# One fused attention and gated-MLP kernel: three late loads moved in the load queue, later transfers planned on one shared wire, and a new order of all work

## The chip, the cores and the metric

The kernel runs on one core of a Trainium2 chip. The core has five engines with a queue of instructions each: TensorE (PE, matrix products into PSUM), VectorE (DVE), ScalarE (ACT), GpSimd (POOL) and SyncE (SP, which here only issues DMA transfers). Each engine runs its instructions in the order in which they are recorded and waits at an instruction until what it needs is there. The metric is the device time of one execution in microseconds (us). The time before is 220.81 us, the median of three runs (220.67 to 221.25).

## What is computed

The input x has 2048 tokens of 512 numbers in bfloat16. The reference, cut to what matters:

```python
x = A_x
xn = _layernorm(x, axis=-1)
s = _A_ref(xn, A_wqkv, A_wo)
g = _silu(_B_ref(xn, B_w_gate, B_w_up, B_w_down))
return x + s * g
```

`_A_ref` is a dilated local attention: q, k and v are products of xn with three 512x512 weights, split into 32 heads of 16; each token attends to 8 tokens, itself and the seven at distances 2, 4, ... 14 before it (those before the start are masked); softmax; then a product with the 512x512 weight wo. `_B_ref` is a gated MLP: gelu(xn w_gate) * (xn w_up), both 512x1792, then a product with the 1792x512 weight w_down, and silu of that.

## The kernel before

The tokens are worked on in four blocks of 512 (j = 0 to 3), each of four tiles of 128. For each block there are these stages:

- Layer normalization on DVE or ACT, and transposition so that the 512 features lie on partitions (tile `xnT`). Block 0 is transposed on PE and copied; blocks 1 to 3 by four DMA transpositions each, issued by SP (line 344, planner's names `copy4` to `copy15`).
- q, k, v: products of `xnT` with the weights. For block 0 by tile of 128 tokens (line 492), for the others in twelve groups of four matmuls of 512 tokens (line 429). ACT evicts each from PSUM (line 440), SP or POOL stores it to DRAM (line 447), and it is loaded again in another layout, heads on partitions (q at line 551, k at 569, v at 587).
- Logits on DVE: products of q with shifted windows of k (`prod`, lines 619 and 692), folds that sum over the 16 numbers of a head (line 705; one large fold in each later block is an adding DMA from POOL, line 714), maximum and difference (727, 733), exp on ACT (746), sum, reciprocal and share on DVE (752 to 762). In block 0 part of the sum runs on PE (`red0`, line 652).
- Values on DVE: four products `pv` a block (line 785), five adds, of which the first two of the four inner ones are adding DMAs (line 808). The result is `o_sb`. It goes to DRAM in four stores (line 941) and comes back transposed as `oT_sb` (line 950).
- Gate and up products: 28 groups of four matmuls a block (line 842), gelu and a copy on ACT (858, 866), the gate product on DVE (line 880, names `geglu`).
- Down products: `y_ps`, 14 matmuls a token tile in cuts of 4, 4, 4 and 2 (line 906); silu on ACT (line 924). Token tiles 0 and 1 share one PSUM tile of two banks, `ps_y`; tiles 2 and 3 take a bank each of the pool "F".
- Output: four matmuls a token tile (line 969), eviction (983), gate by silu (993, or 1020 in the last block), addition of x and store (996 and 1001, or 1026 and 1032).

The PSUM pool "F" has six banks for everything but the two-bank tile "L" (block 0's logits sums and each block's first two y tiles). The products of the gate wait in three buffers of the pool "gl", q, k and v in two buffers each, evicted q, k, v in five ("vst"), hT in one.

The order of the work is not written out. `Kernel` makes a list of about 850 operations with an engine, an estimated duration, needs, buffers and a priority. `schedule` (a list scheduler that runs when the kernel is built) walks them: at each step it picks, over all engines, the operation that can start earliest, ties within 0.05 us going to the lower priority number. The result is one global sequence, and instructions are recorded in it. Durations and costs steer only this order; at run time the engines wait on semaphores for data, buffers and, for each DMA queue, for the transfer eight before it. `slack` adds time to an estimated arrival, and so moves an operation later in the order. The priorities hold a base for each stage and block (`N`, `S`, `V`, `Q`, `F`, `Y`, `O` in `PARAMS`) and, before, a random offset of at most 1.0 from a seed.

Transfers are planned with two wires, one for SP's queue and one for POOL's, by bytes and a rate each, plus a fixed time. The first loads (`loads`) stand at the front of SP's queue: x of block 0 in tiles, q, k and v weights, x of block 1, gate and up weights in halves, x of block 2, the down weights (1792 KB), x of block 3 and the output weights (512 KB each).

Of the kernel before, what the change touches and what calls it, by code (L numbers as in the profile page):

```python
# [16 lines left out]
P = 128  # L17
H = 32
DH = 16
# [9 lines left out]
B, S, D, DF = 1, 2048, 512, 1792  # L29
# [3 lines left out]
TPB = TQ // P  # L33
# [18 lines left out]
PARAMS = dict(  # L52
    sums=(2, 3), ladd=2, ln_act=4, warm=4, slack=1.93, jitter=(8555, 1.0), N=[53.5, -4.6, 83.1, 89.8],
    S=[60.5, 102.4, 90.7, 136.5], V=[57.8, 104.8, 237.5, 47.1], Q=[-7.2, 49.5, -16.0, 37.2],
    F=[1.1, 76.5, 194.5, 255.4], Y=[64.5, 107.9, 241.7, 272.5], O=[82.0, 180.6, 272.0, 282.7], lsum=(0,),
    vsum=(0, 1),
)


class Op:  # L60
    __slots__ = ("name", "eng", "dur", "need", "emit", "take", "use", "prio", "table", "bytes",
                 "start", "done", "end", "n", "slack", "mode")

    def __init__(self, name, eng, dur, need, emit, take=(), use=(), prio=0.0, table=None, nbytes=0,
                 slack=0.0, mode="full"):
# [4 lines left out]
        self.mode = mode  # L70


def schedule(ops, pools):
# [16 lines left out]
    table, mode = None, "full"  # L90
    lanes, lane = {e: [0.0] * 8 for e in ("SP", "POOL")}, {"SP": 0, "POOL": 0}
    wire = {"SP": 0.0, "POOL": 0.0}
    ready = {e: [] for e in clock}
# [6 lines left out]
    while any(ready.values()):  # L100
# [26 lines left out]
        e = o.eng  # L127
# [4 lines left out]
        if o.bytes:  # L132
            clock[e] = t + o.dur
            wire[e] = max(wire[e], t + o.dur / 2) + o.bytes / DMA_RATE[e]
            end = wire[e] + DMA_FIXED + (DMA_CROWDED if e == "POOL" and t < LOADED else 0.0)
            lanes[e][lane[e]] = end
            lane[e] = (lane[e] + 1) % 8
        else:
            if o.table and o.table != table:
                t += TABLE  # L140
                table = o.table
            if e == "PE" and o.mode != mode:
                t += SWITCH
                mode = o.mode
            clock[e] = t + o.dur
            end = clock[e] + LAT[e]
# [19 lines left out]
class Kernel:  # L166
# [52 lines left out]
    def layernorm(self, j):  # L219
        base = self.when("N", j)  # L220
        for tt in range(TPB):
# [117 lines left out]
            if j:  # L339

                def cross(t=t, tt=tt, j=j):
                    if tt == 0:
                        self.new(f"xT{j}", [P, NC, TQ], BF16, "xnT")
                    self.nc.sync.dma_start_transpose(
                        out=self.t[f"xT{j}"][:, :, tt * P : (tt + 1) * P], in_=self.t[f"xn{t}"][:]
                    )

                self.op(f"copy{t}", "SP", 0.8, [f"norm{t}"] + ([f"copy{t - tt}"] if tt else []), cross,
                        take=[("xT", f"xT{j}")] if tt == 0 else [], use=[f"xn{t}", f"xT{j}"], prio=prio,
                        nbytes=P * D * 2)  # L350
                continue
# [63 lines left out]
    def qkv(self, j):  # L415
# [6 lines left out]
        for which, c in groups:  # L422
# [21 lines left out]
            def store(j=j, which=which, c=c, key=key):  # L444
# [7 lines left out]
                    use=["ps_" + key, "st_" + key], prio=0.0)  # L452
            self.op(f"st_{key}", *(("SP", 0.4) if which < 2 else ("POOL", 1.0)), [f"ev_{key}"], store,
                    use=["st_" + key], nbytes=128 * 1024)
            n += 1
# [4 lines left out]
    def halo(self, base):  # L460
# [13 lines left out]
        self.op("halo0", "POOL", 0.2, [], fill, take=[("k", "k0")], use=["k0"], prio=base - 50.0)  # L474
        self.op("st_k0", "SP", 0.5, ["ev_k0_3"], tail, use=["k0"], nbytes=256 * 1024, prio=5.0)

# [5 lines left out]
    def qkv_tiles(self, base):  # L482

        for t in range(TPB):
            for which in range(3):
# [51 lines left out]
                if which == 2:  # L537
                    self.op(f"st_v0_{t}", "POOL", 1.0, [f"ev_v0_{t}"], store, use=[f"vst0_{t}"],
                            nbytes=128 * 1024)
        self.v_loads(0)  # L540

    def q_loads(self, j):
        for tq in range(TPB):

            def load(j=j, tq=tq):
                if tq == 0:
# [10 lines left out]
            self.op(f"ldq{j}_{tq}", "SP", 0.6, need, load, take=[("q", f"q{j}")] if tq == 0 else [],  # L557
                    use=[f"q{j}"], prio=1.0, nbytes=260 * 1024)

    def k_loads(self, j):  # L560
        for tq in range(TPB):

            def load(j=j, tq=tq):
                if tq == 0:
# [12 lines left out]
            self.op(f"ldk{j}_{tq}", "SP", 0.6, need, load, take=[("k", f"k{j}")] if tq == 0 else [],  # L577
                    use=[f"k{j}"], prio=1.0, nbytes=290 * 1024)

    def v_loads(self, j):  # L580
        for tq in range(TPB):
# [14 lines left out]
            self.op(f"ldv{j}_{tq}", "POOL", 1.0, need, load, take=[("v", f"v{j}")] if tq == 0 else [],  # L596
                    use=[f"v{j}"], prio=1.0, nbytes=290 * 1024)

# [82 lines left out]
    def logits(self, j):  # L681
# [3 lines left out]
        for i in range(W // 2):  # L685
# [30 lines left out]
            for n, dur in ((8, 1.135), (4, 0.6), (2, 0.33), (1, 0.33)):  # L716
                if n == 8 and i in self.par["lsum"]:
                    last = self.op(f"fold{j}_{i}_8", "POOL", 1.0, [last], fold_dma, use=[pair],
                                   prio=base + 4 * i + 4.5, nbytes=P * DH * P * 2)
                    continue  # L720
# [57 lines left out]
    def values(self, j):  # L778
# [22 lines left out]
        for i in range(W // 2):  # L801
# [8 lines left out]
            if i in self.par["vsum"]:  # L810
                nm = self.op(f"vadd{j}_0_{i}", "POOL", 1.0, [nm], within_dma, use=[f"pv{j}_{i}"],
                             prio=base + k + 2.5, nbytes=P * DH * P * 2)
# [122 lines left out]
    def turned(self, j):  # L935

        for tq in range(TPB):
# [7 lines left out]

            self.op(f"sto{j}_{tq}", "SP", 0.6, [self.o_ready], store, use=[f"o{j}"], nbytes=340 * 1024, prio=-20.0)

        def load(j=j):
# [4 lines left out]

        self.op(f"ldo{j}", "SP", 0.6, [f"sto{j}_{tq}" for tq in range(TPB)], load, take=[("oT", f"oT{j}")],
                use=[f"oT{j}"], nbytes=512 * 1024, prio=-20.0)

    def out(self, j):
# [31 lines left out]
        if j < NJ - 1:  # L989
# [10 lines left out]
            def store(j=j):  # L1000
# [7 lines left out]
            self.op(f"add{j}", "POOL", 1.0, [f"gate{j}"], add, use=[f"s16{j}"], prio=20.0,  # L1008
                    nbytes=P * TPB * D * 2)
            self.op(f"store{j}", "SP", 0.35, [f"add{j}"], store, use=[f"s16{j}"], nbytes=P * TPB * D * 2)  # L1010
            return
        for tt in range(TPB):
            spans = [(0, 320), (320, D)] if tt == TPB - 1 else [(0, D)]
            for si, (n0, n1) in enumerate(spans):
# [27 lines left out]
                else:  # L1042
# [3 lines left out]
                self.op(f"store{sfx}", "SP", 0.35, [f"add{sfx}"], store, use=[f"s16{j}"],  # L1046
                        nbytes=P * (n1 - n0) * 2)


    def loads(self, src):  # L1050
# [45 lines left out]
        for i, (name, fn, nbytes) in enumerate(seq):  # L1096
            self.op(name, "SP", 0.35, [], fn, prio=-1000.0 + i, nbytes=nbytes)


def plan(par=PARAMS, pools=POOLS, src=(None,) * 6):  # L1100
    k = Kernel(par)
    k.loads(src)
    k.build()
    seed, spread = par["jitter"]
    rng = random.Random(seed)
    for o in k.ops:
        if o.eng in ("PE", "DVE", "ACT") and o.prio > -40.0:
            o.prio += spread * (2.0 * rng.random() - 1.0)
    order, k.slot = schedule(k.ops, pools)
# [108 lines left out]
```

## Time and profile before

| what | value |
|---|---|
| median of three runs | 220.81 us |
| the profiled execution's own time | 220.55 us |
| its span (first to last instruction) | 218.8 us |
| TensorE busy | 208.8 us, 95% |
| VectorE busy | 182.5 us, 83% |
| ScalarE busy | 154.9 us, 71% |
| GpSimd busy | 41.9 us, 19% |
| moved by DMA | 36.02 MB, mean 165 GB/s |
| mean granted clock of TensorE | 0.988 |

The time of an execution holds the span and about 1.7 us around it. All positions in time below are microseconds from the span's start. The busy share of an engine is a mean over stages with different limits, so the stages are looked at one by one: which wait ends last there. "SPq" is SP's queue of DMA issues, "PEld" the load of weights into PE, which overlaps its products. A view of waits names for each engine and line what released it. The chain is followed back from the last instruction, at each step to what released it.

### The profile page before, as it was taken

To read this page: it belongs to the slowest core of one execution; us is meant where nothing else is said; L and a number is where in the kernel's file an instruction comes from. 1 tells how busy PE (TensorE), PEld (TensorE's weight loads), DVE (VectorE), ACT (ScalarE), POOL (GpSimd) and SP (SyncE) were. 2 spreads that over 40 slices of the span, in tenths; PEclk is the share of its full clock that TensorE was granted. 3 is DMA by queue.
4 is the path that set the end of the run, shared out by engine and by line. 5 is a ranking of instruction groups with operands and counts; after the bars stand their busy time and mean duration, and the time that the engine had idled before them with its cause. 6 is when DMAs were issued, how large, how long until landed. Compare 5 with 4: busy or idle time off the path is not lost.

```text
span 218.8 us, 3109 instructions
## 1 busy us (share of the span) xinstructions
PE 208.8 (95%) x1108; PEld 99.3 (45%) x1108; DVE 182.5 (83%) x211; ACT 154.9 (71%) x265; POOL 41.9 (19%) x76
## 2 busy tenths in 40 slices
PE   7999999999399999999999999999999999999991
PEld 2896444444134444444444444444444444444440
DVE  5595995589941999999999999999999999994114
ACT  3588999998766888897734599767644897464351
POOL 5044310203314432240001144120101001101000
PEclk9999999999969999999999999999999999999998
DMA  5999999127999999928245869991075006905552
GB/s 159 363 382 371 323 283 182 26 71 171 234 208 195 256 218 251 166 51 148 96 96 104 222 207 196 193 229 23 16 179 96 0 17 148 217 4 107 104 174 96
DMA packets 48623, 36.02 MB, mean 165 GB/s; under 512 B 29904, under 2 KB 45408, under 8 KB 48608
## 3 DMA queue, kind: packets, MB, share of 16 engines
q1 hardware_dynamic: 44240, 23.99, 44.9%
q0 software_dynamic: 4224, 11.78, 26.4%
q8 instruction: 8, 0.13, 0.3%
q14 instruction: 7, 0.06, 0.2%
q10 hardware_dynamic: 144, 0.07, 0.1%
HBM read 17.44 MB, written 9.47 MB: 123 GB/s over the span
## 4 chain that ended last, share of the span: by engine, by line
DVE 46%; PE 24%; DMA 19%; SPq 4%; issue 3%; ACT 3%; DVEq 0%; ACTq 0%
DVE pv L785 11%; DVE prod L692 8%; PE qkv_ps L429 7%; DVE prod L705 6%; PE g_ps L842 6%; PE u_ps L842 6%; PE qkv_ps L492 5%; DVE hT L880 5%; DMA oT_dram<-o_sb 5%; DVE pv L792 3%; DVE pv L797 3%; DMA kT_dram<-qkv_st 3%; DMA k_sb<-kT_dram 3%; DMA xnT<-xn 2%; DMA out_dram<-s 2%
## 5 line engine op out<-in xcount | busy, mean ns | idle before, releaser
L842 PE MATMUL u_ps<-xnT,wu_sb 128*128 128x512 bf16 x224 | 55.7, 379 | 0.0
L842 PE MATMUL g_ps<-xnT,wg_sb 128*128 128x512 bf16 x224 | 55.5, 379 | 0.0
L906 PE MATMUL y_ps<-wd_sb,hT 128*128 128x512 bf16 x224 | 52.2, 387 | 3.5 <-ACT sil L924 3.5
L866 ACT ACTIVATE hT<-u_ps 128x512 bf16<-128x512 f32 x56 | 33.1, 602 | 12.3 <-PE u_ps L842 12.2
L858 ACT ACTIVATE gl<-g_ps 128x512 bf16<-128x512 f32 x56 | 33.0, 601 | 7.8 <-PE g_ps L842 7.1
L906 PEld LDWEIGHTS <-hT 128*128 128x128 bf16 x224 | 22.3, 100 | 31.2 <-issue 5.9
L785 DVE TENSOR_TENSOR pv<-attn,v_arr 128x4096 bf16<-128x4096 bf16 x16 | 36.3, 2283 | 0.1
L842 PEld LDWEIGHTS <-wu_sb 128*128 128x128 bf16 x224 | 21.9, 98 | 26.4
L842 PEld LDWEIGHTS <-wg_sb 128*128 128x128 bf16 x224 | 21.7, 98 | 25.9 <-issue 0.4
L692 DVE TENSOR_TENSOR prod<-q_sb,k_sb 128x4096 bf16<-128x4096 bf16 x12 | 27.2, 2284 | 4.7 <-DMA k_sb<-kT_dram 4.7
L440 ACT ACTIVATE qkv_st<-qkv_ps 128x512 bf16<-128x512 f32 x36 | 20.4, 603 | 11.5 <-PE qkv_ps L429 8.6
L880 DVE TENSOR_TENSOR hT<-hT,gl 128x1024 bf16<-128x1024 bf16 x28 | 18.9, 680 | 6.3 <-ACT hT L866 6.3
L705 DVE TENSOR_TENSOR prod<-prod 128x1024 bf16<-128x1024 bf16 (+2 forms) x33 | 22.8, 731 | 0.0
L924 ACT ACTIVATE sil<-y_ps 128x512 bf16<-128x512 f32 x16 | 9.3, 597 | 13.9 <-PE y_ps L906 13.9
L808 POOL DMA_DIRECT2D pv<-pv x8 | 7.1, 888 | 58.5 <-DVE pv L785 51.5
L969 PE MATMUL s_ps<-wo_sb,oT_sb 128*128 128x512 bf16 (+2 forms) x68 | 15.1, 367 | 0.2 <-DMA oT_sb<-oT_dram 0.2
L587 POOL DMA_DIRECT2D v_arr<-vT_dram x16 | 10.6, 666 | 16.3 <-DMA vT_dram<-qkv_st 6.6
L983 ACT ACTIVATE s<-s_ps 128x512 bf16<-128x512 f32 x15 | 8.9, 596 | 5.9 <-PE s_ps L969 4.5
L429 PE MATMUL qkv_ps<-xnT,wq_sb 128*128 128x512 bf16 x48 | 11.8, 379 | 0.3 <-DMA xnT<-xn 0.3
L797 DVE TENSOR_TENSOR pv<-pv 128x2048 bf16<-128x2048 bf16 x8 | 9.8, 1221 | 2.8 <-DMA pv<-pv 2.7
L619 DVE TENSOR_TENSOR prod<-q_sb,k_sb 128x1024 bf16<-128x1024 bf16 (+1 forms) x12 | 9.9, 859 | 2.6 <-ACT k_sb L509 2.5
L429 PE MATMUL qkv_ps<-xnT,wk_sb 128*128 128x512 bf16 x48 | 12.0, 379 | 0.0
(89 smaller groups left out, 215.0 us busy)
## 6 DMA issues: line engine op xcount, KB each, us to landing
pv<-pv POOLq DMA_DIRECT2D x8, 512.0 KB, 5.0
v_arr<-vT_dram POOLq DMA_DIRECT2D x16, 142.0 KB, 5.4
oT_dram<-o_sb SPq DMA_DIRECT2D x16, 128.0 KB, 4.3
oT_sb<-oT_dram SPq DMA_DIRECT2D x4, 512.0 KB, 4.4
wg_sb<-in_B_w_gate_dram SPq DMA_DIRECT2D x2, 896.0 KB, 11.1
wu_sb<-in_B_w_up_dram SPq DMA_DIRECT2D x2, 896.0 KB, 13.1
wd_sb<-in_B_w_down_dram SPq DMA_DIRECT2D x1, 1792.0 KB, 20.0
k_sb<-kT_dram SPq DMA_DIRECT2D x12, 142.0 KB, 4.9
```

Of the source, the lines that this page charges most:

```text
L429: self.nc.tensor.matmul(ps[:], lhsT=self.w_sb[which][:, dk, c * P : (c + 1) * P], rhs=self.t[f"xT{j}"][:, dk, :], start=(dk == 0), stop=(d ...
L440: self.nc.scalar.activation(out=st[:], in_=self.t["ps_" + key][:], func=AF.Copy, scale=SCALE if which == 0 else 1.0)
L692: self.nc.vector.tensor_tensor(out=pr[:], in0=self.t[f"q{j}"].unsqueeze(1).to_broadcast([P, 2, DH, P]), in1=win, op=ALU.mult,)
L705: self.nc.vector.tensor_tensor(out=pr[:, :, 0:n, :], in0=pr[:, :, 0:n, :], in1=pr[:, :, n : 2 * n, :], op=ALU.add)
L785: self.nc.vector.tensor_tensor(out=pv[:], in0=self.t[f"at{j}"][:, 2 * i : 2 * i + 2, :].unsqueeze(2).to_broadcast([P, 2, DH, P]), in1=win, ...
L797: self.nc.vector.tensor_tensor(out=out, in0=pa, in1=pb, op=ALU.add)
L842: nc.tensor.matmul(ps[:], lhsT=w[:, dk, fc * P : (fc + 1) * P], rhs=self.t[f"xT{j}"][:, dk, :], start=(dk == 0), stop=(dk == NC - 1),)
L858: self.nc.scalar.activation(out=self.t[f"gl{j}_{pair}"][:, fc % 2, :], in_=self.t[f"ps_g{j}_{fc}"][:], func=AF.Gelu_apprx_tanh,)
L866: self.nc.scalar.activation(out=self.t[f"h{j}"][:, fc, :], in_=self.t[f"ps_u{j}_{fc}"][:], func=AF.Copy)
L880: self.nc.vector.tensor_tensor(out=h, in0=h, in1=self.t[f"gl{j}_{pair}"][:], op=ALU.mult)
L906: nc.tensor.matmul(self.t["ps_" + key][:, 0 : n1 - n0], lhsT=self.t[f"h{j}"][:, fc, tt * P : (tt + 1) * P], rhs=self.wd_sb[:, fc, n0:n1], ...
L969: self.nc.tensor.matmul(ps[:, 0 : n1 - n0], lhsT=self.t[f"oT{j}"][:, c, tt * P : (tt + 1) * P], rhs=self.wo_sb[:, c, n0:n1], start=(c == 0 ...
```

## The change

No operation is added, left out or given to another engine. Five things differ:

1. The last three first loads (down weights, x of block 3, output weights: `late=3`) get a need, normalization 7, and a priority of their own place in the list, where all loads had a priority below -980. The need is known to the planner alone: the loads read no result of that normalization, so in the built kernel they wait for their place in SP's queue. The built order there is: ..., x of block 2, the store of block 0's k tail, `copy4`, down weights, x of block 3, output weights, `copy6`, `copy7`, `copy5`, the stores of block 1's k and q.
2. From 40 us of planned time on, the planner puts all transfers of both queues on one wire, with a fixed piece of work for each kind of transfer (`WORK`), a lag before it and a landing time behind.
3. Planned durations of several DMA issues are changed (0.8 to 1.25 for a transposition, 1.0 to 0.6 or 0.7 on POOL, and so on).
4. The bases of the stages and `slack` (1.93 to 1.65) have new values, and the random offset is replaced by `nudge`, a list with one offset for each operation.
5. So the order changes on every engine. In the first loads, x of token tile 2 now stands ahead of the weights, which come as v, k, q in place of q, k, v. On PE block 0 runs two tiles each of v, k and q ahead of the transpositions of tiles 2 and 3. 20 of block 0's 28 gate and up groups stand ahead of `red0` (23 before), then one y cut and three more groups, then block 1's twelve q, k, v groups; block 1's gate and up groups stand between block 0's y cuts and ahead of block 2's q, k, v. Both token tiles of `ps_y` of block 0 are finished ahead of the first silu. On SP the eight loads of block 1's q and k stand in a row ahead of block 2's transpositions, where before two of these stood among them and two ahead. On DVE block 1's logits end ahead of any product of block 2.

```diff
-LOADED = 42.0
+LOADED = 40.0
 DMA_RATE = {"SP": 325e3, "POOL": 180e3}
+WIRE_LAG = 1.27
+WIRE_LAND = 0.2
+WORK = {"": 0.4, "turn": 0.75, "st": 0.4, "ld": 0.84, "sto": 0.64, "ldo": 2.0, "acc": 2.5, "out": 1.2, "end": 0.05}
...
-    sums=(2, 3), ladd=2, ln_act=4, warm=4, slack=1.93, jitter=(8555, 1.0), N=[53.5, -4.6, 83.1, 89.8],
...
+    sums=(2, 3), ladd=2, ln_act=4, warm=4, slack=1.65, N=[-229.9, -416.4, 944.9, 875.4],
...
+    late=3, vsum=(0, 1),
+    nudge=[
...
         if o.bytes:
             clock[e] = t + o.dur
-            wire[e] = max(wire[e], t + o.dur / 2) + o.bytes / DMA_RATE[e]
-            end = wire[e] + DMA_FIXED + (DMA_CROWDED if e == "POOL" and t < LOADED else 0.0)
+            if t < LOADED:
+                wire[e] = max(wire[e], t + o.dur / 2) + o.bytes / DMA_RATE[e]
+                end = wire[e] + DMA_FIXED + (DMA_CROWDED if e == "POOL" else 0.0)
+            else:
+                begun = t + WIRE_LAG + (0.3 if o.kind == "turn" else o.dur)
+                wire[""] = max(wire[""], begun) + WORK[o.kind]
+                end = wire[""] + WIRE_LAND
...
-                self.op(f"copy{t}", "SP", 0.8, [f"norm{t}"] + ([f"copy{t - tt}"] if tt else []), cross,
+                self.op(f"copy{t}", "SP", 1.25, [f"norm{t}"] + ([f"copy{t - tt}"] if tt else []), cross,
                         take=[("xT", f"xT{j}")] if tt == 0 else [], use=[f"xn{t}", f"xT{j}"], prio=prio,
-                        nbytes=P * D * 2)
+                        nbytes=P * D * 2, kind="turn")
...
         for i, (name, fn, nbytes) in enumerate(seq):
-            self.op(name, "SP", 0.35, [], fn, prio=-1000.0 + i, nbytes=nbytes)
+            late = [f"norm{2 * TPB - 1}"] if i >= len(seq) - self.par["late"] else []
+            self.op(name, "SP", 0.35, late, fn, prio=(0.0 if late else -1000.0) + i, nbytes=nbytes)
...
-    seed, spread = par["jitter"]
-    rng = random.Random(seed)
-    for o in k.ops:
-        if o.eng in ("PE", "DVE", "ACT") and o.prio > -40.0:
-            o.prio += spread * (2.0 * rng.random() - 1.0)
+    if par.get("nudge"):
+        for o, d in zip(k.ops, par["nudge"], strict=True):
+            o.prio += d / 10
```

More of the change, by code (lines that the diff above doesn't have):

```diff
@@ L91, in schedule @@
     lanes, lane = {e: [0.0] * 8 for e in ("SP", "POOL")}, {"SP": 0, "POOL": 0}
-    wire = {"SP": 0.0, "POOL": 0.0}
+    wire = {"SP": 0.0, "POOL": 0.0, "": 0.0}
     ready = {e: [] for e in clock}
@@ L952, in load @@
             )
[L954 to L955 removed]
+        self.op(f"ldo{j}", "SP", 0.4, [f"sto{j}_{tq}" for tq in range(TPB)], load, take=[("oT", f"oT{j}")],
+                use=[f"oT{j}"], nbytes=512 * 1024, prio=-20.0, kind="ldo")
     def out(self, j):
```

40 lines of the change are left out of this document (20 added, 20 removed), and 39 rows, old and new, of the table nudge.

## The prediction

> **What bounds the kernel now.** I read the page first (engine shares, the chain), then stretches of time, then waits, then the chain and timeline where TensorE stops, then landings.
>
> ```profile
> PE 208.8 (95%) x1108; PEld 99.3 (45%) x1108; DVE 182.5 (83%) x211; ACT 154.9 (71%) x265; POOL 41.9 (19%) x76
> ...
> DVE 46%; PE 24%; DMA 19%; SPq 4%; issue 3%; ACT 3%; DVEq 0%; ACTq 0%
> ```
>
> TensorE (PE) is busy 95% of 218.8 us, yet VectorE (DVE) carries most of the chain. Cut into stretches (columns: window; busy us with instructions of PE, PEld, DVE, ACT, POOL; granted clock; DMA share; GB/s):
>
> ```profile
> 56.80:60.30 3.50, 0.03 (x1) 0.00 (x0) 3.47 (x4) 3.47 (x7) 1.94 (x3) 0.97 0.83 195
> 60.30:65.80 5.50, 5.16 (x16) 1.85 (x16) 2.72 (x3) 3.63 (x10) 0.70 (x1) 0.71 1.15 205
> 65.80:71.00 5.20, 5.20 (x25) 2.37 (x26) 0.46 (x2) 3.52 (x7) 2.55 (x5) 1.00 1.35 195
> 71.00:198.00 127.00, 127.00 (x590) 57.59 (x589) 126.66 (x127) 89.49 (x140) 21.44 (x29) 1.00 0.64 135
> 198.00:218.80 20.80, 16.22 (x79) 7.34 (x77) 5.48 (x13) 7.71 (x13) 0.86 (x1) 0.96 0.52 126
> ```
>
> PE stops once, at 56.8, and then runs 16 matmuls at clock 0.71. DVE stops at 66 to 71. From 71 to 198 both are full, so whatever each gains before 71 is gained at the end only if both gain. The waits behind the two stops:
>
> ```profile
> PE y_ps L906 <- ACT sil L924: 3.5, 1, 3.5
> ...
> DVE prod L692 <- DMA k_sb<-kT_dram: 4.7, 1, 4.7
> ```
>
> The first is a matter of order: silu of token tile 0 of block 0 reads one half of the two-bank PSUM tile ps_y0 and is recorded ahead of the second cut of token tile 1, which writes the other half; so PE waits for an ACT that is late. The second is the last load of block 1's k. In the timeline (start, us):
>
> ```profile
> 58.36 1.28 ACT L924 ACT_TABLE_LOAD   x1
> ...
> 60.30 5.16 PE L906 MATMUL y_ps<-wd_sb,hT 128*128 128x512 bf16 x16 [3.47 <-ACT sil L924]
> ```
>
> And the end, in the same view: block 3's o_sb is done at 197.80, is stored, loaded as oT_sb, and the last output matmuls wait for it 0.2 us:
>
> ```profile
> 197.83 2.59 SPq L941 DMA_DIRECT2D oT_dram<-o_sb  x4
> ...
> 210.36 1.90 PE L969 MATMUL s_ps<-wo_sb,oT_sb 128*128 128x512 bf16 x8 [0.21 <-DMA oT_sb<-oT_dram]
> ```
>
> From o_sb to these matmuls it is 12.56 us; with the last matmul at 214.43, 4.4 us of gating, adding and storing end the span.
>
> **The change part by part.** No instruction is added or removed; all is order. A four-matmul group lasts 0.864 us (timeline), an ACT eviction in a row 0.555 (three in 1.74), its statistics 0.61 and 0.70, a normalization 0.74, a table load 1.28.
>
> *The stop at 56.8 goes.* The last group before it ends at 56.67; block 2's first q matmul starts at 65.80. These 9.13 us hold four groups, 3.46 us. In the new order both halves of ps_y0 are finished before the silu is recorded, and block 1's gate and up groups (its xnT is there) stand between. Gain 5.67: 3.63 of stop, 1.55 of half clock, 0.50 before the q matmul. The clock row is the witness: 0.97, 0.71, then 1.00. The Trainium skill, TensorE: Matmul & The Clock Gate, Part 1, says that an idle window of about 3.4 us halves the clock; the stop of 3.63 us agrees. By that rule a new stop under 3.4 us would cost itself alone; by the row alone it could add up to 1.55.
>
> *The first loads.* x tile 2 is issued ahead of the first weight, and v, k, q replace q, k, v. One more 128 KB load ahead: 0.36 us at the page's 363 GB/s, 0.46 by SP's spacing of issues (1.25, 1.71, 2.18). I take 0.46, since SP's queue leads here. Then six tile groups run before the transpositions of tiles 2 and 3, and nothing stands behind these: tile 2's copy on ACT waits for a q eviction (0.60) and lasts 0.60, where before a v group covered it. PE waits about 0.95, less the 0.16 that it waited for wv before: 0.79 (bounds 0 and 1.2, two ACT instructions).
>
> *Down weights, x of block 3, output weights.* They leave the queue's front: 1792+512+512 KB, 7.5 us at 370 GB/s. In SP's new order only one transposition of block 1 stands ahead of them; the other three stand behind. The wait for normalization 7 is in the planner alone; in the queue they stand behind the first transposition, which waits for normalization 4 on ACT. Counting ACT: v eviction to 19.6, table load, four evictions, three normalizations: 25.4. The 6.5 MB ahead have landed by about 22, so the wire idles some 4 us. Loads then run 27.4 to 35, or 36.2 with GpSimd's v loads between; three transpositions at about 1 us each (four issues took 28.97 to 38.2 before, on a full wire) land at 39.4. Down weights land near 34; the first y matmul is at 36.8. PE reaches block 1's k at 6.70 + 10.7 + 1.4 (turns, wait) + 20 groups (17.3) + logit sums 0.65 + four groups (3.5) = 40.25. Cover: 0.85 us. Landings after issue (median us, last column):
>
> ```profile
> wd_sb<-in_B_w_down_dram SPq DMA_DIRECT2D x1, 1792.0 KB, 20.0
> k_sb<-kT_dram SPq DMA_DIRECT2D x12, 142.0 KB, 4.9
> ...
> xnT<-xn SPq DMA_TRANSPOSE x12, 3.3
> ```
>
> Cost taken: 0; ends 0 and about 5, since the slowest transposition of before took 9.1 us from issue to landing, and the last is now issued near 35.
>
> *PSUM around exp of block 0.* Twelve q, k, v groups start at 40.25 while one bank is held by the early y tile and ACT does its table load and exp (1.28 + 1.06, until 43.5). The sixth bank is full at 43.2: PE waits 0.5 (ends 0 and 1.8, by ACT's backlog).
>
> *Block 1's logits.* exp of block 0 ends at 43.5, total at 43.6 (44.59 before). Share 3.2, four pv 8.8, a gate product that waits for ACT until 56.2, four adds, a gate product: o_sb of block 0 at 63.3, against 66.07. The eight q and k loads no longer stand behind block 2's transpositions (L344 at 58.47 for 4.16): they are issued 52 to 57.6 and by the 5.67 us that the chain has for one land at 63.3. DVE's 4.7 us stop becomes 0 to 0.5.
>
> ```profile
> 60.38 5.38 DMA xnT<-xn
> ...
> 86.11 5.67 DMA k_sb<-kT_dram
> ```
>
> *Where the stall goes next.* DVE, 7 us ahead, meets three small waits: a gate product for ACT (0.7), exp of block 1 behind seven evictions (2.0; the old order filled this with a block-2 product), another gate product (0.6). Then block 2's q and k: SP issues one k load ahead of the last q store, so the q loads start near 88.4 and the last is issued at 91.6; with the 4.9 of the row, 96.5 (5.67 gives 97.2, no contention 95.5). Before, this product began at 92.68, but 6.53 us of work that then came after it (totals, share, gate0, a pv, a gate product) is now done: the equal time is 99.2. DVE is 2.7 ahead. From there it was full before (105.1 to o_sb of block 3); two gate products (1.2) now follow o_sb; exp of block 3 is no longer covered by other work and costs about 1.2. o_sb: 96.5 + 105.1 - 6.5 - 1.2 + 1.2 = 195.1; a count along DVE's order gives 195.7. I take 195.4.
>
> *Sum.* PE is free for the last output matmuls at 210.36 - 5.67 - 0.38 + 0.46 + 0.79 + 0.50 + 0.43 (a y group now ahead of them) = 206.5. They wait for oT_sb: 195.4 + 12.5 = 207.9. Four groups, 3.6, and 4.4: 215.9, against 218.8. The profiled execution took 220.55 about its span: 217.65. It lies 0.26 under the median 220.81; in the median's terms 217.9.
>
> **Rivals.**
>
> *Slower: transpositions starve PE.* Three transpositions are issued behind 2.75 MB in the same queue. If the last lands at 39.4 + d, PE stops for d - 0.85 at block 1's first k group, and all of block 1 moves with it; a stop of 3.6 adds 1.5 of half clock as before. The 2.9 us of gain are gone at d = 3.8; with the 9.1 of the slowest landing counted from an issue at 35, d = 4.7 and the time is 220.8 + 2.5 = 223.3. For it: SP's issues stretched to 6.81 us for one load under a full wire. Against: the wire is empty when they start. The Trainium skill, DMA: Bandwidth & Descriptors, Queues, rings and completion order, states that each DMA engine takes a ring's descriptors in order; by that the transpositions cannot overtake, which is what the 39.4 already has, so it speaks for no more than d near 0.
>
> *Banks lock PE in block 3: slower too.* Three gate tiles are computed early and hold three of six banks until products far down DVE's order free their gl buffers; exp of block 3 comes in the same stretch. I count spare times of 0.1 to 1 us. If DVE is 2 us later than counted, PE stops there two or three times for about 1.5, and oT_sb comes later too: about 221.7.
>
> *DVE's lead is eaten: within a few tenths.* If block 2's loads land at 98.5 (the 6.19 us that the chain has for the last o_sb store) and the sum that GpSimd's DMA makes for block 2 (6.2 us, due when DVE asks for it) is 0.7 late, o_sb comes at 197.4 and the time is 220.
>
> *DVE is never late.* PE alone bounds: 206.5 + 3.6 + 4.4 + 2.0 = 216.5; without the two early waits 215.2.
>
> **How the numbers follow.** Forecast (216.8 to 219.3) 0.53; PE alone 0.10; lead eaten 0.17; transpositions 0.10; banks 0.10. About 0.3% (0.7 us) is what a measurement can tell from no change; the lead-eaten case is half faster (219.5 to 220.1), half split between the same and slower. Faster 0.71, same 0.09, slower 0.20. Range: 216.0 leaves out part of the PE-alone case (0.06), 221.9 the slow cases beyond (0.12).
>
> **What the profile after would show.** No PE wait for silu L924's counterpart near 57 and the granted clock at 1.00 from 10 to 200; PE's last matmul near 211.5; no DVE stop over 1 us before block 1's logits, but one of about 2 us for exp of block 1 near 86 and one before block 2's first product; the last transposition of block 1 landed before 40.3; the last output matmuls waiting 1 to 2 us for oT_sb. A PE wait for xnT near 40, or for ACT evictions between 175 and 192, would prove me wrong.

## The result, and the profile after

The kernel after takes 218.65 us (median of six runs, 217.22 to 219.17) against 220.95 for the kernel before on the same chip; the ratio is 0.9887, with a 95% interval of 0.9854 to 0.992. The forecast was 217.9. Run again on the chip of the second set of experiments it took 218.21, ratio 0.9877 (0.9828 to 0.9926). The profiled execution took 218.16, its span is 216.5. Ratios leave out executions more than 1.5% above the fastest of their kernel: of the runs below these are two of the twelve of `a_behind`, 221.93 (the profiled one) and 222.00.

Executions of one kernel differ by 2 us and more, and in the profiled ones up to 2 us of that lies in the first 11 us (last section). So beside the medians I use a ledger: from the start of the first gate matmul to the end of the last matmul, in one profiled execution. Before: 14.92 to 214.43, 199.51 us. After: 18.55 to 211.95, 193.39 us. (In the new order three more q, k, v tile groups of block 0 stand ahead of the first gate matmul, so only kernels with the new order are compared by it with each other.)

The page of after, its engine shares, clock row and chain:

```profile
PE 207.4 (96%) x1108; PEld 99.5 (46%) x1108; DVE 183.3 (85%) x211; ACT 151.4 (70%) x264; POOL 44.2 (20%) x76
...
PEclk9999999999999999999999999999999999999998
...
PE 87%; ACT 4%; DMA 3%; DVE 3%; issue 1%; SPq 0%; DVEq 0%
```

The chain has turned over: before, DVE held 46% of it and PE 24%; now PE holds 87%. PE sets this end. The stretches that answer to the old stop (columns as in the prediction):

```profile
42.00:57.00 15.00, 15.00 (x71) 6.79 (x70) 13.09 (x11) 13.55 (x28) 4.16 (x6) 1.00 0.67 164
57.00:66.00 9.00, 9.00 (x43) 4.08 (x42) 6.45 (x7) 6.77 (x15) 6.16 (x7) 1.00 1.30 184
```

PE is full from 42 to 66, and the granted clock is 1.00: the stop at 56.8 and the half clock behind it are gone. But PE's waits hold two rows that the prediction gave no price (the first and the last here):

```profile
PE qkv_ps L478 <- DMA xnT<-xn: 1.6, 1, 1.6
PE warm_ps L240 <- DVE eps L1214: 1.2, 1, 1.2
PE qkv_ps L541 <- ACT xnT L338: 0.7, 1, 0.7
PE y_ps L955 <- ACT sil L973: 0.7, 1, 0.7
```

The third row is the wait for tile 2's copy that the change brings with it (0.73 at 13.20). The two unpriced ones, in the timeline:

```profile
39.13 1.03 PE L891 MATMUL u_ps<-xnT,wu_sb 128*128 128x512 bf16 x4
41.72 1.89 PE L478 MATMUL qkv_ps<-xnT,wk_sb 128*128 128x512 bf16 x8 [1.56 <-DMA xnT<-xn]
...
163.66 2.11 PE L955 MATMUL y_ps<-wd_sb,hT 128*128 128x512 bf16 x9
166.45 1.89 PE L955 MATMUL y_ps<-wd_sb,hT 128*128 128x512 bf16 x8 [0.69 <-ACT sil L973]
```

A matmul starts 0.216 us after the one ahead of it when nothing holds it. The four at 39.13 are through at 39.99, so the first k group of block 1 came 1.73 us late; its last transposition had only just landed. At 166.45 the matmul starts 1.06 after its predecessor, 0.85 late: in block 2 the silu of token tile 0 is recorded between the first and the second cut of token tile 1, with no other work of PE between the two. It is the old stop again, with another block's names and a quarter of the size. ScalarE is not late here: it starts this silu at 165.81, released by PE's own last matmuls, so PE stands for one silu and the way there and back; all eight profiles with this order show the same 0.85. In the kernel before, blocks 1 and 2 have the same sharing of `ps_y`, but there a cut of token tile 2 is recorded in between, and PE's waits hold no row for it.

What held the transpositions, in stretches of after:

```profile
27.50:34.00 6.50, 6.50 (x32) 2.94 (x31) 6.50 (x7) 6.29 (x16) 0.21 (x1) 1.00 1.01 245
34.00:38.50 4.50, 4.50 (x28) 1.71 (x26) 2.64 (x5) 4.44 (x12) 0.00 (x0) 1.00 1.10 346
38.50:41.00 2.50, 1.66 (x8) 0.57 (x6) 1.36 (x2) 2.48 (x7) 1.01 (x2) 1.00 1.35 172
```

All transfers together moved 245 GB/s until 34, not the 370 that the prediction took. The last of the three late loads, the output weights, was issued at 28.13 and landed 11.4 later, at 39.5; the three transpositions behind it landed at 40.5 to 41.47. GpSimd's last two loads of v are issued at 26.42 and 27.06 and land 5.6 and 7.4 later, at 32.0 and 34.5: they lie in the slow stretch. The down weights, issued at 26.30, landed 10.2 later, at 36.5, just as the first down product started (36.53).

The end, DVE's last sum and the way to the output matmuls:

```profile
195.63 1.23 DVE L846 TENSOR_TENSOR o_sb<-pv 128x2048 bf16<-128x2048 bf16 x1
196.88 2.59 SPq L990 DMA_DIRECT2D oT_dram<-o_sb  x4
201.75 0.37 SPq L999 DMA_DIRECT2D oT_sb<-oT_dram  x1
208.32 1.89 PE L1018 MATMUL s_ps<-wo_sb,oT_sb 128*128 128x512 bf16 x8
```

The load issued at 201.75 lands 4.5 later, at 206.2. The output matmuls start at 208.32 with no wait: 2.1 us to spare.

### The profile page after: what moved, and what is told of

Its sections match the earlier page's. It is cut to its first block, busy times and chain, and to the rows that moved or that the text cites. A ratio compares the mean times of both kernels' runs of the same rounds, so it can differ in the third digit from the quotient of the medians.

```text
span 216.5 us, 3096 instructions
## 1 busy us (share of the span) xinstructions
PE 207.4 (96%) x1108; PEld 99.5 (46%) x1108; DVE 183.3 (85%) x211; ACT 151.4 (70%) x264; POOL 44.2 (20%) x76
## 4 chain that ended last, share of the span: by engine, by line
PE 87%; ACT 4%; DMA 3%; DVE 3%; issue 1%; SPq 0%; DVEq 0%
PE y_ps L955 22%; PE u_ps L891 20%; PE g_ps L891 20%; PE qkv_ps L478 14%; PE s_ps L1018 5%; PE qkv_ps L541 5%; DMA xnT<-xn 2%; DMA x_sb<-in_A_x_dram 1%; ACT gl L907 1%; ACT hT L915 1%; DVE s L1069 1%; ACT junk L347 1%; ACT junk L353 1%; DVE s L1075 1%; DVE stats L413 0%
## 5 line engine op out<-in xcount | busy, mean ns | idle before, releaser
L891 PE MATMUL u_ps<-xnT,wu_sb 128*128 128x512 bf16 x224 | 54.2, 379 | 0.0
L891 PE MATMUL g_ps<-xnT,wg_sb 128*128 128x512 bf16 x224 | 53.9, 379 | 0.0
L955 PE MATMUL y_ps<-wd_sb,hT 128*128 128x512 bf16 x224 | 50.3, 379 | 0.7 <-ACT sil L973 0.7
L907 ACT ACTIVATE gl<-g_ps 128x512 bf16<-128x512 f32 x56 | 32.1, 597 | 15.8 <-PE g_ps L891 11.6
L915 ACT ACTIVATE hT<-u_ps 128x512 bf16<-128x512 f32 x56 | 32.6, 597 | 11.0 <-PE u_ps L891 10.8
L955 PEld LDWEIGHTS <-hT 128*128 128x128 bf16 x224 | 21.8, 98 | 27.6 <-issue 1.0
L489 ACT ACTIVATE qkv_st<-qkv_ps 128x512 bf16<-128x512 f32 x36 | 20.6, 598 | 3.2 <-PE qkv_ps L478 3.1
L973 ACT ACTIVATE sil<-y_ps 128x512 bf16<-128x512 f32 x16 | 8.8, 596 | 14.0 <-PE y_ps L955 13.9
L636 POOL DMA_DIRECT2D v_arr<-vT_dram x16 | 11.3, 802 | 15.1 <-DMA vT_dram<-vst 10.7
L496 POOL DMA_DIRECT2D vT_dram<-qkv_st x12 | 7.1, 597 | 27.0 <-ACT qkv_st L489 26.5
L478 PE MATMUL qkv_ps<-xnT,wq_sb 128*128 128x512 bf16 x48 | 11.3, 379 | 0.0
L478 PE MATMUL qkv_ps<-xnT,wv_sb 128*128 128x512 bf16 x48 | 11.2, 379 | 0.0
## 6 DMA issues: line engine op xcount, KB each, us to landing
wd_sb<-in_B_w_down_dram SPq DMA_DIRECT2D x1, 1792.0 KB, 10.2
```

The costliest lines, as they stand in the source:

```text
L478: self.nc.tensor.matmul(ps[:], lhsT=self.w_sb[which][:, dk, c * P : (c + 1) * P], rhs=self.t[f"xT{j}"][:, dk, :], start=(dk == 0), stop=(d ...
L489: self.nc.scalar.activation(out=st[:], in_=self.t["ps_" + key][:], func=AF.Copy, scale=SCALE if which == 0 else 1.0)
L636: self.nc.gpsimd.dma_start(out=self.t[f"v{j}"][H * tq : H * (tq + 1), :, :], in_=self.vT.rearrange("(h d) s -> h d s", d=DH)[:, :, a : a + ...
L891: nc.tensor.matmul(ps[:], lhsT=w[:, dk, fc * P : (fc + 1) * P], rhs=self.t[f"xT{j}"][:, dk, :], start=(dk == 0), stop=(dk == NC - 1),)
L907: self.nc.scalar.activation(out=self.t[f"gl{j}_{pair}"][:, fc % 2, :], in_=self.t[f"ps_g{j}_{fc}"][:], func=AF.Gelu_apprx_tanh,)
L915: self.nc.scalar.activation(out=self.t[f"h{j}"][:, fc, :], in_=self.t[f"ps_u{j}_{fc}"][:], func=AF.Copy)
```

## The experiments

All edits but two use a helper `moved`, which takes named operations out of the built order and puts them, in the sequence given, ahead of or behind another one. Medians and ratios are against the kernel before on the same chip.

**The late loads back to the front** (the one part of the change that its title names first, undone):

```diff
+    order = moved(order, ["ld_wd", "ld_x3_3", "ld_wo"], behind="ld_x2_2")
```

> The changed kernel with the down weights, x of block 3 and the output weights put back behind x of block 2, ahead of the first transposition; every other order as in the changed kernel. Theory 1 (TensorE alone bounds the changed kernel, and its stop of 1.7 us at 40 comes from three transpositions queued behind these loads): the loads use the wire that idles from 24 to 28, the last transposition lands near 39 as in the kernel before, the stop goes, and the time falls by about 1.7 us to 217.0. Theory 2 (the transpositions are slow because the wire is shared with GpSimd's v loads, wherever the weights stand): the stop stays near 1.7 and the time at 218.6. Theory 3 (the chain over o_sb and oT_sb bounds the end, as the prediction had it): the stop goes, but the time falls by less than 0.5 us, because the last output matmuls then wait for oT_sb.

Measured: 217.15 us (216.41 to 218.53), ratio 0.9801 (0.9751 to 0.9851). Its waits of PE hold no row for xnT at 40:

```profile
PE warm_ps L240 <- DVE eps L1222: 1.2, 1, 1.2
PE qkv_ps L541 <- ACT xnT L338: 0.7, 1, 0.7
PE y_ps L955 <- ACT sil L973: 0.7, 1, 0.7
PE u_ps L891 <- ACT gl L907: 0.3, 1, 0.3
PE tr_ps L436 <- DVE xn L428: 0.2, 1, 0.2
```

The ledger is 192.04, 1.35 under after: the stop of 1.73, less about 0.4 of a new wait for ACT at 74.85. By the ledger the new order is about 1.3 us faster with the loads in front than with them late. So the place of the loads, by itself, lost time in the kernel after. (This execution came to block 1's first k group at 41.6, later than after did, for another reason (last section); but its last transposition, issued at 37.1, landed at 39.86, which is in time for 39.99 too, by a hair.)

**The other side: the transpositions ahead of the loads.**

```diff
+    order = moved(order, ["copy6", "copy7", "copy5"], ahead_of="ld_wd")
```

> The changed kernel with all four transpositions of block 1 ahead of the three loads in SP's queue, nothing else moved. Theory 1: the last transposition lands near 31, so no stop at 40; but the down weights start about 3 us later and land near 38 to 39.5, and the early y cut at 36.5 waits for them 1.5 to 3 us: the stop of 1.7 us moves there, time 218 to 220. Theory 2 (the wire is shared): the loads and transpositions take the same 12 us together whichever comes first, the y cut waits about as long as the k group did, time 218.6.

Measured: 220.61 us (218.23 to 222.00, twelve runs), ratio 0.9943 (0.9906 to 0.9981). Now the down weights, issued at 32.0, are late for the first down product. One wait and three stretches:

```profile
PE y_ps L955 <- DMA wd_sb<-in_B_w_down_dram: 2.0, 1, 2.0
```

```profile
40.20:42.00 1.80, 1.68 (x5) 0.67 (x6) 1.41 (x2) 0.17 (x2) 0.00 (x0) 0.64 1.06 336
42.00:44.00 2.00, 2.00 (x6) 0.76 (x5) 0.00 (x0) 0.36 (x1) 0.00 (x0) 0.50 0.08 26
44.00:46.00 2.00, 1.95 (x10) 0.88 (x9) 0.00 (x0) 1.98 (x5) 0.89 (x2) 0.97 0.00 0
```

A stop of 2.05 us, and 12 matmuls that took 4.29 us in place of 2.59 at the half clock behind it. Together 3.75, less the 1.73 that is gone: 2.0, and the ledger is 195.41, 2.0 above after. The half clock is not in every execution: five of the twelve have the mean clock of this one (0.987 to 0.988), three of them among the ten that the ratio counts; three have 1.00. As long as all three loads are issued in that stretch, whichever of the two stands behind is late.

**Only the megabyte that nobody needs there moved back.** x of block 3 and the output weights go behind the last transposition; the down weights stay.

```diff
+    order = moved(order, ["ld_x3_3", "ld_wo"], behind="copy5")
```

> The changed kernel with x of block 3 and the output weights (1 MB) issued behind the last transposition of block 1; only the down weights stay ahead of it. Theory (the stop at 40 is the time that the late loads hold the wire ahead of the transpositions): 1 MB less is 2.8 us at 370 GB/s, more than the stop of 0.9 to 1.6; TensorE waits under 0.4 for xnT at 40, 217.2 us. Rival (the transpositions themselves are slow beside GpSimd's v loads, whatever stands ahead of them): the wait at 40 stays at 0.8 or more, 218.2 or above.

Measured: 218.19 us (217.50 to 218.85, four runs), ratio 0.9843 (0.98 to 0.9885). The trace bears the theory out; the median by itself does not, it fits the rival (218.2 or above) as well. PE's waits:

```profile
PE warm_ps L240 <- DVE eps L1222: 1.2, 1, 1.2
PE qkv_ps L541 <- ACT xnT L338: 0.7, 1, 0.7
PE y_ps L955 <- ACT sil L973: 0.7, 1, 0.7
PE qkv_ps L541 <- DMA wv_sb<-in_A_wqkv_dram: 0.3, 1, 0.3
```

No wait for xnT; the ledger is 191.95, as with all loads in front. The profiled execution began its first gate matmul at 20.59, 2 us later than after did (last section), which hides the gain in its time; two of the four runs took 217.5 and 217.6, the other two 218.8. A late start could also hide the stop. `a_best2` below settles this, since it has the same split and started on time: its last transposition was issued at 32.3 and landed at 37.1, and the k group started at 39.07 without a wait.

**The silu of block 2.** The second, third and fourth cut of token tile 1 go ahead of the silu.

```diff
+    order = moved(order, [f"mm_y2_1_0_{i}" for i in (1, 2, 3)], ahead_of="silu2_0_0")
```

> The changed kernel with three cuts of y of block 2 (token tile 1) recorded ahead of the silu of token tile 0, which shares their PSUM tile; the order on every engine stays, only the wait between them goes. Theory 1 (TensorE alone bounds): its wait of 0.85 us at 165.6 goes and the time falls by about 0.85 to 217.8. Theory 3 (oT_sb bounds the end): unchanged, 218.6. Theory 4 (ScalarE's silu, now later by about 2 us, delays the gelu of block 3 and PSUM banks with it): the wait comes back before 176 and the time is unchanged.

Measured: 217.98 us (217.07 to 218.26), ratio 0.9834 (0.9791 to 0.9878). The wait at 166 is gone: 55 matmuls of the down product run in a row. But the ledger of its profile is 193.53, no better than after, since another wait, 0.71 from start to start, stands ahead of them:

```profile
152.79 3.63 PE L1018 MATMUL s_ps<-wo_sb,oT_sb 128*128 128x512 bf16 x16 [0.55 <-DMA oT_sb<-oT_dram]
156.26 12.25 PE L955 MATMUL y_ps<-wd_sb,hT 128*128 128x512 bf16 x55
```

oT_sb of block 2 took 12.7 us from issue to landing here, 11.3 in after, where it landed at 151.9 for matmuls at 152.22. The spare time at this place is 0.3 us, not the 2.1 of block 3. The edit lies behind this place, so it did not make the load late: the same load took 11.2 to 13.0 us in the profiles of the new order. The median lies 0.2 to 0.7 under the two medians of after, so this run does not settle what the 0.85 is worth in the time.

**The transposition of x tile 2, earlier.** It goes ahead of the first q groups and its copy ahead of their eviction, to take away the 0.73 at 13.20.

```diff
+    order = moved(order, ["turn2"], ahead_of="mm_q0_t0")
+    order = moved(order, ["copy2"], ahead_of="ev_q0_0")
```

> The changed kernel with the transposition of tile 2 one group earlier on TensorE and its copy one eviction earlier on ScalarE. Theory 1: the wait of 0.7 us at 12.5 goes and everything up to the transpositions of block 1 comes 0.7 to 0.9 earlier, the normalizations and with them the DMA transpositions too, so the stop at 40 stays as it is: time 217.8 to 218.0. Rival: the transpositions' landing hangs on the wire and not on the normalizations, the stop at 40 grows by the same 0.8, and the time stays at 218.6.

Measured: 217.47 us (217.30 to 217.97), ratio 0.9819 (0.9777 to 0.9862). The row is gone from PE's waits, the first gate matmul starts at 18.00 in place of 18.55, and the ledger behind it is after's (193.21): the stop at 40 stays, at 1.4.

**Three edits at once, and with the other cure for the loads.** `a_best` is the first, fourth and fifth edit together; `a_best2` has the split in place of the loads in front. For comparison the kernel after itself, `after2`, ran beside the former.

> The changed kernel as it is, so that the kernels below are compared with it on one chip. Expected: 218.6 us, ratio to the kernel before 0.988; TensorE waits of about 1.5 for xnT at 40 and of 0.7 for a silu at 166 in its profile.

> Three edits of the changed kernel together: the three late loads go back to the front of SP's queue, the second cut of block 2's token tile 1 is finished ahead of the first silu, and the transposition of x tile 2 with its copy goes ahead of the first q groups. Theory 1 (TensorE's own work alone sets the end; the DVE chain to oT_sb has about 2 us to spare): the three stops of 1.73, 0.85 and about 0.7 add up, 218.6 - 3.3 = 215.3, no TensorE wait above 0.5 between 10 and 200. Rival (the prediction's forecast: DVE and oT_sb bound the end as soon as TensorE is free): DVE's work does not get shorter, so the last output matmuls wait for oT_sb about 1 us and the time stays at 216.3 or above.

> The edit of a_split, the silu of block 2 recorded behind both token tiles, and the earlier transposition of x tile 2, together. By the run of the three edits with the loads in front (216.84, with waits of 0.2 to 0.4 for oT_sb at 151 and for ACT in place of the stops) oT_sb of block 2 is the next limit: 216.5 to 217.0 and such a wait near 151. If the stops added up without a next limit: 215.3.

Measured: after2 218.21 us (217.40 to 220.49); a_best 216.84 (215.97 to 217.28), ratio 0.9798 (0.9761 to 0.9835); a_best2 215.75 (215.55 to 217.77), ratio 0.975 (0.971 to 0.9789), the fastest here. Of the 3.3 us that the three stops are worth, a_best won 1.4 over after2, which ran beside it. Neither theory holds as it stood: the stops do not add up in full, and yet the time is not held where the forecast said. a_best2 came out below the 216.5 to 217.0 that was expected and 0.45 above the 215.3 of full addition; by the ratios (0.975 against 0.9877 and 0.9887) it won 2.8 to 3.0 of the 3.3. Its ledger is 191.64: of the 2.58 that the stops at 40 and 166 are worth in it, it keeps 1.75 (a_best, 192.16, keeps 1.23). So the next limit that its expectation was built on is there, but takes less. The chain of a_best2, and the matmul at which DVE's work comes into it:

```profile
PE 36%; DVE 18%; ACT 18%; DMA 16%; issue 5%; SPq 5%; DVEq 0%; ACTq 0%
```

```profile
150.19 1.04 PE L1018 MATMUL s_ps<-wo_sb,oT_sb 128*128 128x512 bf16 x4 [0.17 <-DMA oT_sb<-oT_dram]
```

PE has fallen from 87% to 36%, and the chain passes through block 2's oT_sb: its matmuls start 0.55 after their predecessor, 0.33 late. Small waits for ACT (0.3 near 40 in a_best, whose last transposition landed at 39.89 only) make up more. The last output matmuls still wait for nothing.

**One part alone, in the kernel before: the silu behind three cuts of token tile 1** (the fourth cut stands behind block 2's q, k, v groups either way).

```diff
+    order = moved(order, [f"mm_y0_1_0_{i}" for i in (1, 2)], ahead_of="silu0_0_0")
```

> The kernel before with one edit: the second cut of block 0's token tile 1 is finished ahead of the first silu, nothing else. Theory 1 (the stop at 56.8 goes only because there is other work between; block 2's xnT lands at 65.8 whatever PE does): PE runs through to about 60.3 and stops there 5.5 us for xnT instead; 0 gained, or up to 1.5 lost if half clock follows: 220.8 to 222.5. Rival (the stop is the silu's alone): 3.5 to 5.7 faster, 215.2 to 217.5.

Measured: 223.19 us (222.63 to 224.66), ratio 1.0114 (1.0059 to 1.0168): slower, and 0.7 above the 222.5 that was allowed for. The stretches:

```profile
56.50:60.00 3.50, 3.47 (x17) 1.37 (x14) 3.47 (x4) 3.47 (x7) 1.95 (x3) 1.00 0.85 200
60.00:66.00 6.00, 0.38 (x1) 0.14 (x2) 2.99 (x3) 3.64 (x10) 0.70 (x1) 0.79 1.13 197
66.00:71.00 5.00, 5.00 (x15) 1.85 (x14) 0.50 (x1) 2.21 (x5) 1.91 (x4) 0.57 1.16 159
```

PE runs through 56.8 and then stands 5.65 us, until block 2's first q matmul at 65.62: that group waits for xnT, whose last transposition lands at 65.53, whatever PE does before. The half clock behind the longer stop costs more too: the 16 matmuls from 65.62 (15 of them recorded) took 5.72 us in place of 3.46, 2.3 lost, where before the 16 from 60.30 lost 1.55. The silu alone was not the stop; what the change had to bring was work to lie between.

**One part alone, in the kernel before: the loads late.** They stand behind `copy4`, as in after.

```diff
+    order = moved(order, ["ld_wd", "ld_x3_3", "ld_wo"], behind="copy4")
```

> The kernel before with one edit: down weights, x of block 3 and output weights are issued behind copy4 as in the kernel after, all else in the old order. Theory 1 (the late loads by themselves bring nothing, the stops at 56.8 and of DVE at 66 are of the order of other work): within 1 us of the kernel before, or slower by up to 2 where block 1's transpositions or the first down product are late. Rival (the empty wire early in the kernel is what gains): faster by 1 us or more.

Measured: 221.78 us (220.50 to 223.43), ratio 1.002 (0.9988 to 1.0053): nothing to be told from no change. PE's and DVE's stops are the old ones, 3.5 us for the silu and 4.8 for k:

```profile
PE y_ps L906 <- ACT sil L924: 3.5, 1, 3.5
...
PE qkv_ps L429 <- DMA xnT<-xn: 0.4, 1, 0.4
...
DVE prod L692 <- DMA k_sb<-kT_dram: 4.8, 1, 4.8
```

So the late loads gain nothing alone, and in the new order they lose (a_front). The whole gain is that of the new order of the other work; which piece of it gains how much was tried for the silu alone.

**DVE made later, ahead of block 3's last sum of values.** Three copies, and then twelve, of a tile that nobody reads, added to after:

```diff
     for o in order:
+        if o.name == "vadd3_1_2":
+            for t in (12, 13, 14):  # a_dve4: (12, 13, 14) * 4
+                nc.vector.tensor_copy(out=k.junk[:], in_=k.x_sb[:, t, :])
         o.emit()
```

> The changed kernel with three extra DVE copies (about 1 us together) just ahead of the second of block 3's last sums of pv, so o_sb of block 3 comes 1 us later and nothing else changes. Theory (TensorE sets the end, oT_sb of block 3 lands about 2 us before it is needed): unchanged, 218.2 to 218.6. Rival (the forecast: o_sb and oT_sb set the end): slower by 1.0.

> As a_dve, with twelve copies (about 4.1 us). Theory: the spare time of 2.1 us is used up, the last output matmuls wait about 2 us for oT_sb, slower by 2.0 (220.4). Rival (o_sb sets the end already): slower by 4.1 (222.5).

Measured: a_dve 218.77 us (218.66 to 220.18), ratio 0.9871 (0.9827 to 0.9914); a_dve4 221.73 (220.98 to 223.71, ten runs), ratio 1.0038 (1.0004 to 1.0071). The copies took 0.94 and 3.90 us. The first is no slower than after by what these runs can tell, and its last output matmuls do not wait: so o_sb of block 3 did not set the end. The second is 3.1 to 3.5 us slower, between the two theories (2.0 and 4.1). Its trace shows why it is above 2.0:

```profile
201.40 1.02 PE L891 MATMUL g_ps<-xnT,wg_sb 128*128 128x512 bf16 x4 [1.23 <-ACT gl L907]
202.26 8.80 PE L955 MATMUL y_ps<-wd_sb,hT 128*128 128x512 bf16 x39
212.02 3.64 PE L1018 MATMUL s_ps<-wo_sb,oT_sb 128*128 128x512 bf16 x20 [0.97 <-DMA oT_sb<-oT_dram]
```

A late DVE reaches PE on two ways. By oT_sb, 0.97; and, 10 us sooner, by the gate products: they come late behind the copies, hold their gl buffers, ACT cannot evict, and PE finds no bank: 1.23. That is the mechanism of the rival on banks, here at a price of its own. The two starts are late by 1.39 and 1.13, 2.5 in all; what is left to the measured 3.1 to 3.5 I leave open.

## Why the prediction came out as it did

The direction and the main term were right, by the mechanism given; the time came out 0.75 above the forecast. That it came so near is partly luck. The forecast was set by a path, oT_sb at 207.9, that ended 1.7 us earlier (206.2), and PE, which did set the end, came 1.8 us later than forecast (208.32 for 206.5), mainly because of two waits that were priced at nothing. Of the prediction's own signs four did not come out: there is a PE wait for xnT near 40, which was to prove it wrong; the last transposition of block 1 landed at 41.47, not before 40.3; DVE stood 2.5 us, not under 1, before block 1's logits; and the last output matmuls do not wait for oT_sb.

- *The stop at 56.8 goes: right.* PE is full from 42 to 66 at clock 1.00. That the gain needs the work between, not the order of the silu alone, is shown by b_silu.
- *Down weights, x of block 3, output weights, "Cost taken: 0": the term that was mis-sized.* It cost 1.73 (1.09 in after2's execution, where the first k group started 1.30 after its predecessor). The step that failed is the wire: 370 GB/s and an end at 36.2, where the trace has 245 until 34 and the last load landing at 39.5. So d was 2.1 and not 0 (41.47 for 39.4). Of that the cover takes 0.85; PE came 0.26 sooner than written (39.99 for 40.25), and from the landing to the first matmul it is 0.25: 1.73. It is the rival "transpositions starve PE" at half its strength; a_front, a_split and a_best2 show that the bytes ahead of the transpositions are the cause. Why those bytes moved at 245 is open: the rate rises at 34, about when GpSimd's last load of v lands (34.5), but no run moved these loads.
- *A stop that was not in the list:* the silu of block 2, 0.85. The prediction counted block 0's silu out and did not look for the same pattern in the three other blocks, though the new order was there to be read. The pattern that costs is the narrower one: no work of PE between the last write ahead of the silu and the next behind it.
- *The first loads:* 0.46 taken, 0.23 measured, and not by the load: the first v matmul starts at 6.24, as the first q matmul did before (6.25), but the first eight lie 88 ns apart in place of 59, because the first five ran at half rate (last section). In after2 the first v matmul did wait 0.30 for its weights. The wait for tile 2's copy 0.79, measured 0.73. *PSUM around exp of block 0:* 0.50 taken, 0 measured; PE, held by xnT, came late to it.
- The sum for PE: 206.5 + 1.73 + 0.85 - 0.23 - 0.50 - 0.06 = 208.3, and the last output matmuls start at 208.32. The sum closes. (The 0.38 that the prediction's sum takes off without a word is the wait for oT_sb at 210.36 counted from start to start.)
- *Block 1's logits:* o_sb of block 0 at 63.3, measured 62.97. Block 1's k at 63.3, measured 65.47: the last of its loads was issued at 59.93, not 57.6, so DVE stood 2.5 us where 0 to 0.5 was written. *Where the stall goes next:* exp of block 1 held DVE 1.45 at 88.13 (2.0 written), and block 2's first product ran at 96.33 (96.5 written). o_sb of block 3 ended at 196.86 against 195.4: 1.5 late.
- *The end: wrong in its limit.* "They wait for oT_sb: 195.4 + 12.5 = 207.9." The 12.5 was the row of before, 12.56; in after it is 9.4 until oT_sb is there (206.2). The missing 3 us are in the stores. In before GpSimd's adding DMA for the output (512 KB) was issued at 199.23, ahead of the last of the four o_sb stores, which then took 6.19:

```profile
199.10 0.64 SPq L941
199.78 6.19 DMA oT_dram<-o_sb
206.16 0.36 SPq L950
```

  In after that add is issued at 199.72, behind the last store, and the load follows 4.9 us after o_sb's end in place of 8.4. All fourteen profiles agree: in the three with the old order there (before, b_silu, b_late) the add is issued 0.55 ahead of the last store, which takes 5.9 to 6.2; in the eleven others 0.9 behind it, and that store takes 2.7 to 3.4. No run moved the add alone, so it is argued and not shown that this is the cause. I had read the 12.56 as the price of the path; it seems to have held another transfer's turn on the wire. So the rival "DVE is never late" (PE alone bounds, 216.5) is what happened at the end, with PE's 1.8 on top: 218.3, against 218.16 of the profiled execution. It does not hold with much room: 2.1 us at block 3, 0.3 at block 2, and there a_silu, a_best and a_best2 ran into it.

A word on half clock. The prediction set a rule of the Trainium skill (TensorE: Matmul & The Clock Gate, Part 1: an idle window of about 3.4 us halves the clock) against the row of before. The new stop of 1.73 us left the clock at 1.00, as the rule has it; but in a_behind a stop of 2.05 us, with eight 32-column matmuls just ahead of it, was followed by 0.50 in the profiled execution. There the measurement decides: a stop under 3.4 us can halve the clock. What the profiles with half clock in the middle share is its length. Stretches of before, b_silu and a_behind, each exactly as long as the half clock lasted (b_late is as before):

```profile
60.06:63.47 3.41, 3.17 (x8) 1.17 (x8) 0.79 (x1) 3.28 (x10) 0.70 (x1) 0.50 1.16 229
63.43:70.26 6.83, 4.64 (x11) 1.61 (x12) 2.45 (x2) 2.23 (x6) 1.23 (x2) 0.50 1.27 172
40.69:44.10 3.41, 3.41 (x10) 1.22 (x8) 0.92 (x1) 0.46 (x1) 0.00 (x0) 0.50 0.45 143
```

It lasts 3.41 us or twice that. A stop costs, behind itself, half of the time that PE runs in it: 1.6 in before (from 60.30), 2.3 in b_silu (from 65.62), 1.7 in a_behind. In a_behind the half clock began at 40.69, and PE had been running again since 40.32. In the 3.41 us ahead of 40.69 PE had stood for 2.05 and had run the 32-column matmuls for another 0.6. So it may be how idle a whole stretch of this length was that counts, and not the stop alone; one case does not show it.

## What to carry to other kernels

Look for an instruction that shares a buffer with a reader recorded ahead of it in every block of the new order, not only where the old profile shows the stop, and ask whether other work of the same engine stands between the two. A row of a path that has DMAs in it holds whatever else was on the wire, so before it is moved, ask which transfer stood in it. A transfer that is put "late" to clear the queue stands ahead of something else there; move only the bytes that are not needed soon (here x of block 3 and the output weights, behind the transpositions).

## What the runs showed of the hardware that I had not expected

The first groups of an execution run at full rate or at half, in kernels that have the same instructions up to there. Timeline and a stretch of a_front, then of after2:

```profile
6.38 3.59 PE L541 MATMUL qkv_ps<-xnT,wv_sb 128*128 128x128 bf16 x32
```

```profile
6.00:10.00 4.00, 4.00 (x39) 3.78 (x38) 1.79 (x5) 0.90 (x3) 0.79 (x1) 1.00 1.09 361
```

```profile
6.53 1.96 PE L541 MATMUL qkv_ps<-xnT,wv_sb 128*128 128x128 bf16 x32 [0.30 <-DMA wv_sb<-in_A_wqkv_dram]
```

```profile
6.00:10.00 4.00, 3.70 (x66) 3.53 (x65) 1.89 (x6) 2.00 (x5) 1.40 (x2) 1.00 1.10 360
```

39 matmuls in the first against 66, with the clock row at 1.00 in both. By the starts of the matmuls the spacing is 107 ns until 10.0 to 10.7 in a_front, a_behind, a_split, a_dve and a_dve4, and 56 ns from 6.1 to 6.9 on in the other profiles, before among them. The first gate matmul of those five starts at 20.2 to 20.6, that of after, after2 and a_silu at 18.4 to 18.6: some 1.7 to 2.2 us of an execution, as large as an effect that was looked for, and it shows in no row of waits. The Trainium skill (TensorE: Matmul & The Clock Gate, Part 1) says that the activity window runs freely and so the turn to full clock moves by about 500 ns; here it moved by 3 us and more, which is nearer to one whole window of the 3.4 us that the page gives. That it is one window is not shown.
